# Paired table products, extra dense products and a new order in a gated mix of attention and a state-space convolution

## The chip, the cores and the metric

One Trainium2 chip, one of its cores. The metric is the device time of one execution in microseconds, the median of several runs. The core has five engines that run their own instruction streams and wait for each other by semaphores: TensorE (PE; its weight loads are shown apart as PEld), VectorE (DVE), ScalarE (ACT), GpSimd (POOL) and SyncE (SP). In this kernel POOL and SP do little but issue DMAs.

## What is computed

Two branches over the same input x (2048 x 512) are mixed by a gate per token. Cut to what matters here:

```python
# branch A: 32 heads of 16, 4 segments of 512 tokens
for s in range(4):
    logits = einsum('bhqd,bhkd->bhqk', q[s], k[s]) * scale + mask   # causal
    a_dot = softmax(logits) @ v[s]
    a_mem = (phi(q[s]) @ M) / (phi(q[s]) @ z + 1e-6)
    o[s] = g * a_mem + (1 - g) * a_dot
    M = M + phi(k[s]).T @ v[s];  z = z + phi(k[s]).sum()
a = o @ wo
# branch B: per channel d of 512, a kernel of 2048 taps from 128 complex modes, then a long convolution
l = arange(2048).astype(bfloat16)          # many l fall together
K = einsum('dn,dnl,dn->dl', C, exp(dt * A * l), dt * B).real
y = irfft(rfft(x, 4096) * rfft(K, 4096))[:2048] + x * Dskip
out = sigmoid(x @ gate_w) * a + (1 - sigmoid(x @ gate_w)) * y
```

## The kernel before

**A planner writes the order.** The kernel is built as a list of operations, each with an engine, an estimated cost, tiles that it reads and writes and a key. A list scheduler (`schedule`) takes on each engine, among the operations that can start within 0.12 us, the one with the lowest key; `ORDER` holds for each tag a number that is added to the key, and a second that is added only where DVE competes for an eviction. An eviction (`evac`, lines 324, 325, 327, 328) may go to ACT or DVE. All instructions are then written out engine by engine, with no loops. Every product goes through one helper, line 820.

**Attention.** 4 segments, 4 head groups of 8 heads each, and two halves of a head group: 32 calls of `group`, each with 5 score steps, 160 in all. A score step writes 1024 columns in two PSUM banks (0 and 1, or 2 and 3); ACT takes the exponential of all of it (line 1169). The causal mask of the diagonal blocks is set in one of two ways, a bit in `MASKS` for each step: by two more products, one per bank, that add `negm` through the identity, or by a DVE product with `mask01` after the exponential (line 1178). A step has 2 or 4 diagonal blocks of 128.

**Tables.** The taps of the state-space kernel are made from powers: 20 powers `F` and 32 powers `G` per mode and channel, so that each of 640 exponents is one of F plus one of G. `tables(c)` handles 128 channels, four times over. DVE makes F and G by complex multiplication (lines 1328, 1330, 1333). Then, per channel, PE multiplies G's 32 columns (stationary) with F's 20 columns (moving), summed over the modes, the real and the imaginary part in turn. Four channels stand side by side in the array's columns, so each product is 32 x 20. Results gather in one PSUM bank for each half of the channels, are evicted into `kex`, and four DMAs per table carry `kex` into `KTT`, which has exponents in its partitions.

**Convolution.** A transform of 4096 points in two levels. The first level of x (`x_level1`) is a product with `W1T` and goes through DRAM (`scr_Z`). In `tail`, 16 steps `K0` to `K15` each take the transform of the taps (a product of a matrix from DRAM with `KTT`, so all four tables must be there), that of x, multiply them on DVE (lines 1425, 1427, 1430) and transform back into `V2`. When all of `V2` is there, the last stage `fin` multiplies it with `G2T`, adds branch A, scales and writes out (line 327).

**Memory.** PSUM banks 4 to 7 serve one bank at a time for everything but the scores. `kex` shares its place with `pb2`, a parameter that the preparation reads last in `cbB` (line 936).

Of the kernel before, what the change touches and what calls it, by code (L numbers as in the profile page):

```python
# [16 lines left out]
    'c_ident': (-302.654696, 118.5323), 'c_mk': (25.0776717, 31.1201), 'c_negm': (117.240337, 15.88946),  # L17
    'c_mask': (82.9696732, 148.73681), 'c_ones': (219.06097, 69.01982), 'c_W1': (101.972009, -1.91191),
    'c_G2': (152.510402, 64.12832), 'ld0': (-159.6066, -3.90904), 'ld1': (-178.483329, -24.17737),
    'ld2': (-92.104013, -32.87557), 'ld3': (-67.6677276, 9.94046), 'ld4': (-16.8975543, -9.33976),  # L20
    'ld5': (-4.87843354, -20.81767), 'ldt': (-255.221528, 18.97994), 'ldw0.3': (-120.015437, 20.25449),
    'ldw0.4': (-107.069287, 54.02795), 'ldw0.5': (-74.7706898, 55.68128), 'ldw50': (143.580885, 71.64248),
    'ldbd': (146.873282, -3.63178), 'ldc': (75.9548493, -139.44835), 'prep': (241.088944, 76.53782),
    'xT0': (-135.794939, 94.16918), 'powA0': (-118.34783, 47.94242), 'powA1': (293.056234, 56.59733),
    'powA2': (35.605867, 26.1545), 'powA3': (85.9672701, 3.55388), 'powA4': (-134.9878, 64.48103),
    'powA5': (-26.1625064, 59.29796), 'powA6': (-133.006553, -36.0664), 'powA7': (-142.410857, 92.25773),
    'powA8': (-143.096642, 54.65219), 'powA9': (-10.832777, 2.7911), 'cbA': (-135.566534, 76.23563),
    'powB0': (-38.6484402, 86.47076), 'powB1': (5.73197339, 19.09463), 'powB2': (-13.5842481, 50.52935),
    'powB3': (-134.626625, -55.3453), 'powB4': (-158.321758, -62.26012), 'powB5': (-189.375726, 81.95324),
    'powB6': (-80.3854645, -2.33938), 'powB7': (-23.5296877, 39.40937), 'powB8': (-69.1011372, 80.90111),  # L30
    'powB9': (-110.631611, 11.18354), 'cbB': (-43.7416241, -8.34436), 'gate0': (-83.6885532, -16.32166),
    'gate': (1.11235274, 54.68591), 'proj0.0': (-19.4170356, -12.54463), 'tok0': (-79.3938344, 28.87985),
    'state0': (2.03704365, 1.9988), 'grp0.0.0': (-9.77190791, 56.39033), 'grp0.0.1': (-15.5684214, 42.32006),
    'oph0.0': (16.6476846, 20.40017), 'proj0.1': (-31.4882721, 74.16452), 'grp0.1.0': (-22.0475879, 127.40729),
    'grp0.1.1': (-23.8762151, 61.87469), 'oph0.1': (-9.68776635, -98.76067), 'proj0.2': (13.8209713, 33.73148),
    'grp0.2.0': (-3.0729207, -42.9295), 'grp0.2.1': (-4.41502647, 85.93088), 'oph0.2': (-0.110628858, -73.44253),
    'proj0.3': (-3.65051527, 62.72309), 'grp0.3.0': (-157.898249, 69.86549), 'grp0.3.1': (15.8097506, 82.05476),
    'oph0.3': (1.58288994, 45.63335), 'oproj0': (-119.328043, -32.2024), 'xT1': (152.351944, 17.87594),
    'proj1.0': (9.25225381, 119.56925), 'tok1': (-10.2534902, 33.782), 'state1': (2.65910208, -104.20105),
    'grp1.0.0': (-90.77533, -81.81367), 'grp1.0.1': (2.11773201, -114.61486), 'oph1.0': (-2.73170943, -41.40325),  # L40
    'proj1.1': (1.88542876, 58.71674), 'grp1.1.0': (-50.654272, 32.17712), 'grp1.1.1': (2.9233842, 75.51506),
    'oph1.1': (-10.8350984, -95.48593), 'proj1.2': (1.82372045, 0.09674), 'grp1.2.0': (-40.190034, 101.48513),
    'grp1.2.1': (6.26606409, 118.92692), 'oph1.2': (-0.686318884, -116.61307), 'proj1.3': (0.240651948, 30.33776),
    'grp1.3.0': (-46.8631087, 31.58558), 'grp1.3.1': (4.26113506, 92.65595), 'oph1.3': (16.5142754, -29.00959),
    'oproj1': (-191.3713, -3.8356), 'xT2': (96.7803542, 126.17717), 'proj2.0': (2.03309827, 56.77169),
    'tok2': (4.1651971, -119.61949), 'state2': (5.77674239, -0.78865), 'grp2.0.0': (-34.2653109, -9.07765),
    'grp2.0.1': (-5.67836684, 97.22657), 'oph2.0': (-250.752907, -56.23876), 'proj2.1': (6.5976729, 122.63846),
    'grp2.1.0': (-4.50294478, 30.38303), 'grp2.1.1': (4.81855669, 106.57043), 'oph2.1': (15.6722872, -167.79793),
    'proj2.2': (-0.107249989, 90.02738), 'grp2.2.0': (-195.487509, 48.11696), 'grp2.2.1': (-5.26881311, 86.02262),
    'oph2.2': (10.7493513, -113.28868), 'proj2.3': (-7.49951321, 95.76044), 'grp2.3.0': (5.83724795, 81.21215),  # L50
    'grp2.3.1': (-32.6003357, 74.62712), 'oph2.3': (-34.0930078, -105.98926), 'oproj2': (-42.4160159, -7.99807),
    'xT3': (290.268696, 20.01374), 'proj3.0': (0.804501688, 7.58942), 'tok3': (5.05705523, 9.43832),
    'grp3.0.0': (-16.6209468, 115.71971), 'grp3.0.1': (-94.3400298, 75.95984), 'oph3.0': (34.3743725, -53.14357),
    'proj3.1': (-5.34871522, 74.39357), 'grp3.1.0': (31.8837621, -11.25205), 'grp3.1.1': (-311.171354, -14.40604),
    'oph3.1': (-107.203104, -69.86356), 'proj3.2': (72.9991952, 27.09956), 'grp3.2.0': (20.1657102, -6.85936),
    'grp3.2.1': (-59.0699755, -14.4919), 'oph3.2': (88.4879918, -147.86965), 'proj3.3': (79.119397, 97.40507),
    'grp3.3.0': (5.32990942, 126.86441), 'grp3.3.1': (61.7741135, -22.60438), 'oph3.3': (-130.287319, -60.50239),
    'oproj3': (-33.6345043, -45.3022), 'tab0': (-0.0762501383, 297.60803), 'tab1': (-3.85305439, 267.74954),
    'tab2': (-0.288638216, 266.94455), 'tab3': (9.72332812, 324.53498), 'xl1': (-134.058337, -22.9888),
    'tailload': (-94.6594205, 59.19368), 'K0': (-16.3376241, 5.32994), 'K1': (44.0845545, -26.15755),  # L60
    'K2': (9.34286849, 3.42233), 'K3': (45.356053, 32.70617), 'K4': (39.7158986, -80.36254),
    'K5': (59.226848, -13.36243), 'K6': (-175.798043, 23.12264), 'K7': (-52.4250027, -83.01271),
    'K8': (-81.0202091, -26.97997), 'K9': (70.2758069, 29.6753), 'K10': (11.2349379, 25.06385),
    'K11': (-5.3357892, -30.98575), 'K12': (-72.5533468, 4.35854), 'K13': (83.6417633, 0.11429),
    'K14': (94.4918388, -109.55134), 'K15': (132.562985, 53.83523), 'fin': (-85.9153477, -15.31372),
    'pre0': (169.976104, -25.42423), 'fin0': (91.9347751, 60.72191), 'pre1': (-73.3504102, -61.54381),
    'fin1': (115.799027, 117.99035), 'fin2': (125.104546, 66.48059), 'fin3': (213.962257, 170.74892),
}
MASKS = [2, 0, 0, 0, 0, 0, 0, 0, 0, 28, 0, 0, 0, 1, 0, 0, 16, 16, 14, 4, 0, 28, 0, 1, 3, 15, 31, 31, 15, 13, 26, 20]
# [566 lines left out]
def dft_const():  # L636
    lq = (np_bf16_bits(np.arange(2048, dtype=np.float32)).astype(np.uint32) << 16).view(np.float32).astype(np.int64)
    where = {}
    for f, fe in enumerate(F_EXP):
        for g, ge in enumerate(G_EXP):  # L640
            assert fe + ge not in where
            where[fe + ge] = (f % 5, 4 * g + f // 5)
    assert set(lq[1:].tolist()) == set(where)
    D = np.zeros((128, 16, 5, 2, 128))
    t = np.arange(16)[:, None, None]
    pi = np.arange(2)[None, :, None]
    q = np.arange(64)[None, None, :]
    f = (2 * t + pi + 64 * q).reshape(16, 128)
    for l in range(1, 2048):
        kt, r = where[int(lq[l])]  # L650
        ph = 2 * np.pi * (((2 * f + 1) * l) % 8192) / 8192
        D[r, :, kt, 0, :] += np.cos(ph)
        D[r, :, kt, 1, :] -= np.sin(ph)
    return D


def build_kernel(nc, A_x, A_wq, A_wk, A_wv, A_wo, A_beta, B_A_re, B_A_im, B_B_re, B_B_im,
                 B_C_re, B_C_im, B_log_dt, B_Dskip, gate_w, out):
    with contextlib.ExitStack() as es:
# [102 lines left out]
        kexP = mkpool("kex", 1280, 2)  # L762
# [3 lines left out]
        assert a <= 207 * 1024, a  # L766

        pbP = mkpool("pb", 1024, 2)
# [9 lines left out]
        pb2P = mkpool("pb2", 1024, 1, 0)  # L778
        a = GP.addr
# [182 lines left out]
        def x_level1(xjP, zsP):  # L962
            S.tag = "xl1"
            for qd in range(4):
# [3 lines left out]
                for bl in range(4):  # L968
# [3 lines left out]
                    def f(e, P=P, xj=xj, bl=bl):  # L972
                        for hf in range(2):
                            i = mm(e, ap(P, hf * 512, n=512), ap(W1T, hf * 128, n=128), ap(xj, bl * 512, n=512), True, True)
# [159 lines left out]
        def group(s, hg, gi):  # L1134
# [12 lines left out]
            for si, ent in enumerate(slots):  # L1147
# [3 lines left out]
                def f(e, P=P, ent=ent, md=md):  # L1151
                    dg = {0: [], 1: []}
                    for (hh, J, bk, off) in ent:
# [13 lines left out]
                o_ = op("PE", (0.28 if len(ent) == 2 else 0.36) if md else (0.38 if len(ent) == 2 else 0.63), f, r=[qT, kT, ko, ident, negm], w=[P], acq=[pT], act=0.08 + (0 if md else 0.0533 * len(ent)))  # L1167
# [131 lines left out]
        def tables(c):  # L1299
# [62 lines left out]
            for hf in range(2):  # L1362
# [210 lines left out]
```

## Time and profile before

| | |
|---|---|
| median of 8 runs | 361.13 us |
| lowest, highest | 354.11, 365.34 us |
| the profiled execution | 360.26 us |
| its span, first to last instruction | 358.5 us |
| instructions | 8296 |
| PE busy | 301.8 us, 3409 products |
| weight loads | 126.1 us, 3409 |
| DVE busy | 275.0 us, 667 |
| ACT busy | 286.3 us, 387 |
| mean granted clock of TensorE | 0.931 |

Busy time of PE is from modelled ends, so a busy PE need not be at its peak. The granted clock is the share of full speed that the chip allowed TensorE; it has its own row. In a row of a group, the number after x is the count, then come the busy time in us, the mean of one in ns, the idle time before them, and what ended most of that idle time. "Issue" as a releaser means that nothing in the profile explains the wait. The chain of waits is followed back from the last instruction to what released each step. Most of it is attention and tables up to about 240 us, then attention of the last segment mixed with the 16 steps of the tail up to 338 us, then the last stage.

### The profile page before, as it was taken

The page shows a single profiled execution, that of the slowest core. Times are in us where ns is not written, and L with a number is a line of the kernel's source. Part 1 is how long each engine was busy: PE and PEld are TensorE (multiplying, and loading weights), DVE is VectorE, ACT ScalarE, POOL GpSimd, SP SyncE. Part 2 cuts the span into 40 slices and gives each one's busy share as a digit, 9 for nine tenths or more (in the row PEclk, how much of TensorE's full clock was granted, in tenths as well). Part 3 has the DMA queues.
Part 4 walks back from the last instruction along what each step waited for, and adds up shares of the span by engine and source line. Part 5 has one row for each costly group of instructions (what it writes and reads, how often), then busy time and mean ns, then how long its engine had stood idle before and what let it go on. Part 6 is the DMA issues. An engine that isn't in the chain of part 4 may idle for free.

```text
span 358.5 us, 8296 instructions
## 1 busy us (share of the span) xinstructions
PE 301.8 (84%) x3409; PEld 126.1 (35%) x3409; DVE 275.0 (77%) x667; ACT 286.3 (80%) x387; POOL 17.2 (5%) x39
## 2 busy tenths in 40 slices
PE   0569887788849989989798999969999999999581
PEld 0223332233424433534335433443343333344240
DVE  2689999999848997399996999913686787986320
ACT  2688999999928998989998898926899768665472
POOL 2000000000100000000020000000001121100000
PEclk9996998599988996999999999995899999999997
DMA  7968021023692555410024210251126657443342
GB/s 145 195 147 121 1 90 29 3 58 120 192 123 90 152 143 188 140 35 15 2 87 125 64 44 16 46 165 35 37 49 229 216 152 237 140 121 89 106 155 92
DMA packets 43118, 37.56 MB, mean 105 GB/s; under 512 B 30569, under 2 KB 35945, under 8 KB 42217
## 3 DMA queue, kind: packets, MB, share of 16 engines
q1 hardware_dynamic: 39016, 22.18, 24.6%
q0 software_dynamic: 2720, 13.63, 12.4%
q10 hardware_dynamic: 1344, 1.21, 1.7%
q8 instruction: 27, 0.44, 0.5%
q14 instruction: 11, 0.08, 0.1%
HBM read 17.74 MB, written 9.44 MB: 76 GB/s over the span
## 4 chain that ended last, share of the span: by engine, by line
PE 35%; DVE 31%; ACT 23%; DMA 4%; issue 4%; SPq 0%
PE psum L820 35%; ACT sb L1169 12%; ACT sb L324 6%; DVE sb L325 4%; DVE sb L1333 4%; DVE sb L1330 4%; DVE sb L1328 4%; DMA sb<-in_B_A_im_dram 2%; ACT sb L327 2%; DVE sb L1232 1%; DVE sb L1430 1%; DVE sb L1252 1%; DVE sb L1425 1%; DMA sb<-scr_obuf 1%; DMA sb<-sb 1%
## 5 line engine op out<-in xcount | busy, mean ns | idle before, releaser
L820 PE MATMUL psum<-sb 128*32 128x20 bf16 (+13 forms) x3233 | 290.8, 278 | 48.3 <-DMA sb<-in_A_x_dram 12.6
L820 PEld LDWEIGHTS psum<-sb 128*128 128x128 bf16 (+4 forms) x3233 | 115.7, 97 | 219.1 <-issue 91.1
L1169 ACT ACTIVATE sb<-psum 128x1024 bf16<-128x1024 f32 x160 | 157.7, 1037 | 9.8 <-PE psum L820 9.3
L324 ACT ACTIVATE sb<-psum 128x512 bf16<-128x512 f32 (+2 forms) x134 | 97.8, 754 | 38.7 <-PE psum L820 37.9
L325 DVE CAST sb<-psum 128x512 bf16<-128x512 f32 (+2 forms) x39 | 35.0, 897 | 17.2 <-PE psum L820 17.1
L1328 DVE TENSOR_TENSOR sb<-sb 128x512 bf16<-128x512 bf16 (+3 forms) x52 | 34.3, 664 | 0.1
L1333 DVE TENSOR_TENSOR sb<-sb 128x512 bf16<-128x512 bf16 (+3 forms) x52 | 34.0, 664 | 0.1
L1330 DVE TENSOR_TENSOR sb<-sb 128x512 bf16<-128x512 bf16 (+3 forms) x52 | 33.9, 664 | 0.0
L1178 DVE TENSOR_TENSOR sb<-sb 128x512 bf16<-128x512 bf16 (+1 forms) x43 | 15.8, 372 | 5.3 <-ACT sb L1169 5.2
L324 ACT ACTIVATE sb<-sb 128x256 bf16<-128x256 bf16 (+1 forms) x32 | 15.4, 499 | 1.1 <-DVE sb L904 1.0
L1425 DVE TENSOR_TENSOR sb<-sb 128x1024 bf16<-128x1024 bf16 x16 | 10.8, 683 | 6.5 <-ACT sb L324 5.2
L1229 DVE RECIPROCAL sb<-psum 128x32 f32<-128x32 bf16 x16 | 5.7, 355 | 11.6 <-PE psum L1226 11.6
L1430 DVE TENSOR_TENSOR sb<-sb 128x512 bf16<-128x512 bf16 x32 | 13.2, 418 | 0.6
L317 POOL DMA_DIRECT2D sb<-c_D x16 | 8.6, 537 | 95.3 <-PE psum L820 70.4
L327 ACT ACTIVATE sb<-psum,sb 128x512 bf16<-128x512 f32 x13 | 8.6, 687 | 4.8 <-PE psum L820 4.8
L1427 DVE TENSOR_TENSOR sb<-sb 128x1024 bf16<-128x1024 bf16 x16 | 10.9, 684 | 0.2 <-ACT sb L324 0.2
L1232 DVE TENSOR_TENSOR sb<-psum,sb 128x512 bf16<-128x512 bf16 x16 | 10.9, 684 | 0.0
L1226 PE MATMUL psum<-sb 128*128 128x128 bf16 x128 | 10.3, 226 | 0.1
L1252 DVE TENSOR_TENSOR sb<-psum,sb 128x256 bf16<-128x256 f32 x24 | 9.2, 417 | 0.1
L1226 PEld LDWEIGHTS psum<-sb 128*128 128x128 bf16 x128 | 7.8, 100 | 2.9 <-issue 1.1
L325 DVE COPY sb<-sb 128x256 bf16<-128x256 bf16 x17 | 4.0, 250 | 5.9 <-PE psum L820 5.9
L1125 ACT ACTIVATE sb<-sb 128x512 bf16<-128x512 bf16 x12 | 8.0, 662 | 0.1
(71 smaller groups left out, 143.5 us busy)
## 6 DMA issues: line engine op xcount, KB each, us to landing
sb<-c_D POOLq DMA_DIRECT2D x16, 320.0 KB, 4.4
scr_Z<-sb SPq DMA_DIRECT2D x16, 256.0 KB, 2.0
sb<-scr_Z POOLq DMA_DIRECT2D x4, 1024.0 KB, 5.5
sb<-sb SPq DMA_DIRECT2D x15, 256.0 KB
sb<-in_A_x_dram POOLq DMA_DIRECT2D x4, 512.0 KB, 5.1
scr_obuf<-sb SPq DMA_DIRECT2D x12, 128.0 KB, 1.9
scr_abuf<-sb SPq DMA_DIRECT2D x12, 128.0 KB, 1.8
sb<-scr_abuf SPq DMA_DIRECT2D x3, 512.0 KB, 6.0
```

Source lines behind the costliest of these rows:

```text
L324: fa = lambda e: e.activation(dst(), src(), ACT.Copy)
L325: fd = lambda e: e.tensor_copy(dst(), src())
L327: fa = lambda e: e.activation(dst(), src(), ACT.Copy, scale=scale())
L820: mm = lambda e, o_, l, r_, st, sp, **kw: e.matmul(o_, lhsT=l, rhs=r_, start=st, stop=sp, skip_group_check=True, **kw)
L1169: op("ACT", c_act(1024), lambda e, P=P, pT=pT: e.activation(ap(pT, n=1024), ap(P, n=1024), ACT.Exp, scale=0.25), r=[P], w=[pT])
L1178: o_ = op("DVE", c_tt(128 * len(offs)), lambda e, pT=pT, dims=dims: e.tensor_tensor(ap(pT, dims=dims + [[1, 128]]), ap(pT, dims=dims + [[1 ...
L1226: i = e.transpose(ap(P, tb * 256 + gi * 128, n=128), ap(ra[gi], tb * 128, n=128), ap(ident, n=128))
L1232: op("DVE", c_dps(512), lambda e: e.tensor_tensor(ap(o1, dims=[[128, 4], [16, 8], [1, 16]]), ap(P, dims=[[256, 4], [32, 8], [1, 16]]), ap( ...
L1328: op("DVE", ct, lambda e: e.tensor_tensor(run(tile, ne, dst, 1), run(tile, ne, src, sstep), pwv(0), ALU.mult), r=rd + [pw], w=wr + [tile])
L1330: op("DVE", ct, lambda e: e.tensor_tensor(run(t2, n, 0, 1), run(tile, ne, src, sstep), pwv(1), ALU.mult), r=rd + [pw], w=[t2])
L1333: op("DVE", max(c_tt(256 * n), 0.4), lambda e: e.tensor_tensor(D_(), D_(), ap(t2, n * 128, [[-n * 128, 2], [2 * n, 64], [1, 2 * n]]), ALU. ...
L1430: op("DVE", c_tt(512), lambda e, Y=Y, Tt=Tt, c=c, alu=alu: e.tensor_tensor(ap(Y, 512 * c, n=512), ap(Y, 512 * c, n=512), ap(Tt, 512 * c, n ...
```

## The change

Four things are changed.

1. `tables` multiplies two channels at once: 64 columns of G (two channels) with 40 columns of F (the same two channels), two such products side by side in the array. Of each 64 x 40 result only the two blocks of 32 x 20 on its diagonal are used. A table's 32 steps go into three PSUM banks (12, 12 and 8 steps) and not two, each with a tag and key of its own, and groups of four steps have keys 0.6 apart. The eviction takes all 40 columns; the DMA picks the blocks. `kex` is twice as large, and `pb` moves into its place. So that channels lie as the pairs need them, three constants and the moving operands of the products with `W1T` and `G2T` are rearranged.
2. `FILLS`: 44 score steps begin with one more product, 128 rows of `kT` by 512 columns of `qT`, whose result is overwritten by the score products that follow.
3. `MASKS` has other bits: 71 steps are masked on DVE, before 43.
4. Every number in `ORDER` is new.

```diff
 ORDER = {
-    'c_ident': (-302.654696, 118.5323), 'c_mk': (25.0776717, 31.1201), 'c_negm': (117.240337, 15.88946),
...
+    'c_ident': (-730.92885, 77.11646), 'c_mk': (-104.472085, 70.23437), 'c_negm': (83.1023139, 57.29774),
...
+    'oproj3': (-215.379276, -234.39235), 'tab0': (-3.31108379, 556.81397), 'tm0.0': (-175.547175, 364.57757),
...
-MASKS = [2, 0, 0, 0, 0, 0, 0, 0, 0, 28, 0, 0, 0, 1, 0, 0, 16, 16, 14, 4, 0, 28, 0, 1, 3, 15, 31, 31, 15, 13, 26, 20]
+MASKS = [1, 0, 0, 0, 0, 0, 8, 1, 29, 1, 17, 18, 0, 31, 18, 7, 26, 3, 8, 31, 4, 26, 31, 23, 10, 13, 30, 25, 30, 23, 20, 14]
+FILLS = [0, 0, 2, 0, 10, 15, 0, 11, 29, 1, 20, 16, 27, 16, 25, 20, 0, 0, 0, 0, 14, 2, 5, 0, 0, 4, 10, 17, 4, 0, 13, 1]
...
-            where[fe + ge] = (f % 5, 4 * g + f // 5)
+            where[fe + ge] = (f // 4, 4 * g + f % 4)
...
-        kexP = mkpool("kex", 1280, 2)
+        kexP = mkpool("kex", 2560, 2)
...
-        pbP = mkpool("pb", 1024, 2)
...
         pb2P = mkpool("pb2", 1024, 1, 0)
+        pbP = mkpool("pb", 1024, 2, 0)
...
-                            i = mm(e, ap(P, hf * 512, n=512), ap(W1T, hf * 128, n=128), ap(xj, bl * 512, n=512), True, True)
+                            i = mm(e, ap(P, hf * 512, n=512), ap(W1T, hf * 128, n=128), ap(xj, bl * 512, [[2, 2], [4, 128], [1, 2]]), True, True)
...
+                    if FILLS[gidx] >> si & 1:
+                        mm(e, ap(P, n=512), ap(kT, n=128), ap(qT, n=512), True, True)
...
-            for hf in range(2):
+            for pc, (lo_, n_) in enumerate(((0, 12), (12, 12), (24, 8))):
+                S.tag = "tm%d.%d" % (c, pc)
                 P = S.ps()
-                for sl0 in range(0, 16, 4):
-                    def f(e, P=P, hf=hf, sl0=sl0):
-                        for sl in range(sl0, sl0 + 4):
+                for s0 in range(0, n_, 4):
+                    S.key = k0 + KEYS[3] * 0.8 + 8 * pc + 0.6 * s0
+
+                    def f(e, P=P, lo_=lo_, s0=s0):
+                        for sl in range(s0, s0 + 4):
                             for cc in range(2):
-                                for dq in range(4):
-                                    dl = 32 * dq + 16 * hf + sl
-                                    i = mm(e, ap(P, sl * NF, n=NF, p0=32 * dq, np_=32), ap(G, (1 - cc) * GPL + (dl // 2) * 2 * NG + dl % 2, [[2, NG]]),
-                                           ap(F, cc * FPL + (dl // 2) * 2 * NF + dl % 2, [[2, NF]]), cc == 0, cc == 1, tile_position=(0, 32 * dq))
+                                for ct in range(2):
+                                    j, par = 32 * ct + (lo_ + sl) // 2 * 2, sl % 2
+                                    i = mm(e, ap(P, sl * 2 * NF, n=2 * NF, p0=64 * ct, np_=64), ap(G, (1 - cc) * GPL + j * 2 * NG + par, [[2, 2 * NG]]),
+                                           ap(F, cc * FPL + j * 2 * NF + par, [[2, 2 * NF]]), cc == 0, cc == 1, tile_position=(0, 64 * ct))
                         return i
...
-                S.evac(lambda hf=hf: ap(kex, 16 * hf, [[32, NF], [1, 16]]), lambda P=P: ap(P, dims=[[1, NF], [NF, 16]]), 320, r=[P], pw=[kex])
+                S.evac(lambda lo_=lo_, n_=n_: ap(kex, lo_, [[32, 10], [320, 4], [1, n_]]), lambda P=P, n_=n_: ap(P, dims=[[4, 10], [1, 4], [2 * NF, n_]]), 40 * n_, r=[P], pw=[kex])
...
-                      lambda dq=dq: ap(kex, n=640, p0=32 * dq, np_=32), 40960, r=[kex], pw=[KTT], rate=60e3, issue=0.6)
+                      lambda dq=dq: ap(kex, dq % 2 * 160, [[320, 4], [1, 160]], p0=32 * dq, np_=32), 40960, r=[kex], pw=[KTT], rate=60e3, issue=0.6)
...
-                            i = mm(e, ap(P, n=512), ap(G2T, kt * 128, n=128), ap(V2, (b4 * 2 + kt) * 512, n=512), False, kt == 1)
+                            i = mm(e, ap(P, n=512), ap(G2T, kt * 128, n=128), ap(V2, (b4 * 2 + kt) * 512, [[2, 128], [256, 2], [1, 2]]), False, kt == 1)
```

## The prediction

> **What bounds it now.** I read the page first: share by engine, the 40 slices, the chain of waits by line. No single engine is the limit (PE 84%, ACT 80%, DVE 77%), so the question is which stage waits for what. Then the groups by shape on PE, the chain in order of time, and stages cut out by time.
>
> ```profile
> PE   0569887788849989989798999969999999999581
> ...
> DVE  2689999999848997399996999913686787986320
> ACT  2688999999928998989998898926899768665472
> ...
> PEclk9996998599988996999999999995899999999997
> ...
> PE 35%; DVE 31%; ACT 23%; DMA 4%; issue 4%; SPq 0%
> ```
>
> A digit covers 9.0 us. Up to slice 26 (234 us) DVE and ACT are nearly always full. Counted from 0, there are two holes in both: slice 11 (DVE 4, ACT 2 tenths) and slice 26 (1 and 2), each followed by a granted clock under full. The chain names the holes (start, length, what was on it):
>
> ```profile
> 98.65 1.65 PE psum L820 x126
> 100.30 4.82 issue
> 105.12 8.65 PE psum L820 x40
> ...
> 134.45 10.72 PE psum L820 x151
> ...
> 227.39 10.65 PE psum L820 x297
> 238.04 3.48 issue
> 241.52 4.58 PE psum L820 x31
> 246.10 0.97 PE psum L1226 x8
> 247.07 10.01 PE psum L820 x45
> ```
>
> "Issue" is PE waiting for nothing the trace shows, straight after a burst of hundreds of products. Groups by shape say what they are:
>
> ```profile
> L820 PE MATMUL psum<-sb 128*32 128x20 bf16 x1024 | 12.0, 176 | 4.3 <-issue 4.0 <-DVE sb L1333 0.2
> ```
>
> These are the table products. By the records of this line they run in bursts of 32, some 6 to 10 ns apart, 8.4 us in all. So they cost PE little as work, but they are 2048 of its 6818 instructions (one weight load and one product each). The page's q8 row has 27 instruction blocks in 0.44 MB, so 16 KB and about 253 PE instructions each. A burst uses up a block in about 1.2 us. In the packet records the block that ended the first stall moved from 102.75 to 103.71, and PE went on at 105.12; for the second it moved from 239.14 to 240.15, and PE went on at 241.52. I read both stalls as PE out of instructions.
>
> The stages (PE busy, weight loads, DVE, ACT, POOL, granted clock, DMA share, GB/s):
>
> ```profile
> 59.87:70.11 10.24, 7.77 (x50) 2.37 (x50) 10.24 (x25) 10.24 (x17) 0.00 (x0) 0.50 0.07 15
> 97.42:104.25 6.83, 2.23 (x141) 1.42 (x140) 3.37 (x9) 3.55 (x7) 0.53 (x1) 1.00 1.10 140
> 104.25:111.07 6.82, 5.95 (x21) 1.92 (x22) 4.49 (x13) 2.84 (x4) 0.00 (x0) 0.50 0.21 63
> ...
> 134.97:141.80 6.83, 6.83 (x65) 1.98 (x62) 5.46 (x17) 5.12 (x8) 0.53 (x1) 0.50 0.53 162
> ...
> 240.78:254.43 13.65, 12.91 (x84) 4.63 (x85) 4.78 (x15) 8.08 (x10) 0.00 (x0) 0.50 0.09 23
> 342.60:350.80 8.20, 8.20 (x39) 3.50 (x36) 2.25 (x3) 7.46 (x12) 0.00 (x0) 1.00 0.51 190
> ```
>
> The clock is 1.00 or 0.50 and changes in steps of 3.41 us. I weighed each 3.41 us by the array it used (columns streamed times the share of rows and columns, at 0.21 us for a full product of 512, from 39 in 8.20 us above). Each fall to 0.50 between 25 and 255 us came after a step with at most 1.31 us of such dense work (0.38, 1.31, 0.00, 1.05, 0.09); the lowest step that kept the clock had 1.20. Attention before 100 us lives at 1.2 to 1.9, just above.
>
> **The holes, as prices.** A, 238.04 to 254.43: the stall 3.48 plus half of the 12.91 us at half clock, 9.9. B, 100.30 to 111.07: 4.82 plus half of 5.95, 7.8. C, 134.97 to 141.80: half of 6.83, 3.4. D, 59.87 to 70.11: ACT is full there; PE is on the chain only from 67.36, so half of 2.75, 1.4. Sum 22.5.
>
> **Table products in pairs (`tables`).** 1024 products of 32x20 become 512 of 64x40, half of each result unused. At 6 to 10 ns each they cost 3.1 to 5.1 us against 8.4; on the chain stand 1.65 us and some 3.5 us of the 10.65, so about 2.5 us go. PE's instructions fall by 1024, and the eight emitted groups of a table hold 32 instructions, not 64, with keys 0.6 apart per four products. Masks and fills included, PE has 6818 - 1024 + 88 - 112 = 5770. Two of four tables (142 to 151 us, 188 to 196 us) already ran without a stall at twice the density, so I take both stalls as gone, and with them the empty steps that cost the clock: A and B in full, 17.7. If PE were not short of instructions, only the halved bursts would remain.
>
> The Trainium skill speaks against this: "Runtime: NRT & Kernel Launch", section "Instruction fetch mechanics", says that streaming in 16 KiB blocks is mostly hidden behind issue. The trace shows two stalls, 8.3 us, so I follow the trace; by the page the forecast would be 8.3 higher.
>
> **Evictions of the tables.** Two of 320 elements become 480, 480, 320. Rows: 320 takes 439 ns on ACT, 512 takes 618; 480 lies at 588 in between. A table goes from 0.88 to 1.62 us, four of them +2.9 us. The strip of 320 bytes that each DMA to `KTT` now reads changes neither count nor size (16, 40 KB, 2.2 us to landing); three of four tables land long before use, so nothing. `pb` under `kex` adds a wait on `cbB`, ended by 76.5 us (last L936), before the first product at 92: nothing; `pb2` already made it.
>
> **Masks.** 43 steps masked on DVE become 71: 13 more with two blocks (285 ns, L1178 128x256) and 15 with four (424 ns): 3.7 + 6.4 = 10.1 us more DVE. PE loses 56 products and 13 x 0.107 + 15 x 0.213 = 4.6 us of dense work. By segment +2, +15, +14, -3.
>
> **Fills.** 44 more 128x512 products, 10, 18, 6, 10 by segment, 0.21 us each at full clock: 9.4 us. In segments 0 to 2 the score step waits for ACT's Exp (1037 ns each, 158 us in all) and the fill lies under it: nothing; it delays the score products behind it by 0.21 us, up to 7.3 us for the 34 if that cover were gone. In segment 3 PE is the bound (9.0 of 9.0 us in most slices): 10 x 0.21 = 2.1, and three masks back on PE, 0.5. What they buy: D and C are falls without a stall. Segments 0 and 1 gain dense work net, segment 2 loses some 1.0 us. I take half of C and D, 2.4.
>
> "TensorE: Matmul & The Clock Gate", Part 1, lets the clock fall after an idle window of 3.4 us. Before 59.87 PE was busy 2.69 of 3.41 us and fell all the same, so the trace goes by dense work; by the page fills buy nothing, 2.4 less gain.
>
> **Where the added work lands.** In 36 to 99, 117 to 135 and 153 to 234 us DVE is 97% and ACT 95% busy. 13.0 us more, shared by choosing the engine of the evictions, is 6.5; all on DVE alone 13; in the holes, nothing. I take 6.5: it is nearest to those rows. Cap: in 99 to 117 and 135 to 153 the two engines idle 23.9 us together, so B and C can give back at most 12.
>
> **Rearranged columns.** The products with `W1T` and `G2T` now read pairs of elements 8 or 512 bytes apart. No row has that. The table products read single elements at 4 byte steps, 32 of them (four abreast) in 0.2 us, so 20 columns in at most 25 ns: at worst a third of full rate, 0.43 us more per 512. The 32 with `G2T` lie on the last 9 us: 0 to 13.6 us. Below zero is excluded, since the same columns stream. I take 0: `KTT` is read in pieces too and PE's pace there is normal.
>
> **New order.** All keys change; no row prices that. It moves DMAs on SP and POOL as well, and it may open new steps under 1.3. I take one more fall of D's kind, 1.4; bounds are none and C's 3.4 twice.
>
> **Sum.** On the profiled 360.26 us (span 358.5): -17.7 - 2.4 - 2.5 + 6.5 + 2.6 + 1.4 = -12.1, so 348.2. The median shown, 361.13, is 0.9 higher: 349.
>
> **Rivals.**
> 1. No change: the gaps close, but DVE takes all 13.0 us, and C and D stay with two falls of C's kind instead of one of D's: -17.7 - 2.5 + 13.0 + 2.6 + 6.8 = +2.2, about 361 to 363; with half of that, 357 and up. For it: DVE is on 31% of the chain, with runs of 20 us and more. Against: the evictions can move, and 39 on DVE (35.0 us) is more than enough to move.
> 2. Slower: a spread group keeps its PSUM bank, one of the four (4 to 7) for everything but the scores, from its first product to its eviction. 12 such holds; PE's waits for evictions on these banks (L324, L325, L1232, L1252) are 22 us between 36 and 241. If one missing bank doubles them while it is held for T, the price is 22 x 12T/205 = 1.3T. From T = 12 us it eats the forecast and more; at 14 us, 18 more, 367. For it: banks are waited for. Against: keys inside a group differ by 2.4 at most, where a whole attention group has 11.
> 3. Slower: rearranged reads at their bound, 349 + 13.6 = 363, and with the fills uncovered 370.
> 4. The change doesn't do what it says: the stalls come from busy DMA queues (share 1.10 in 97 to 104 us), not density; A and B keep their 8.3: 357.
>
> **Chances.** Forecast, with rival 4 mostly below the bound, 0.72; rival 1, 0.12; rival 2, 0.10; rival 3, 0.06. A measurement tells about 1% (3.6 us) from no change. Faster 0.72, same 0.12, slower 0.16. Range: everything recovered and all additions hidden is 361.1 - 22.5 = 338.6; the upper end takes in rivals 4 and 1 and the bound of the reads, 364. The forecast's own cases lie at 338 to 357.
>
> **What would show it.** Right: no "issue" piece over 1 us on the chain, slices like 11 and 26 gone from DVE and ACT, clock 1.00 after the table products; table products x512; ACT and DVE together near 574 us. Wrong: stalls elsewhere with the clock full; half clock in segment 2, where fills are few; waits of PE for L324 and L325 clearly over 22 us; the last products with `G2T` more than 0.21 us apart.

## The result and the profile after

The changed kernel takes 360.37 us (median of 11 runs, 358.46 to 365.34), the kernel before 358.15 us (median of 32). The ratio is 1.0108, 95% interval 1.0066 to 1.0151: slower by about 1%, where 349 us and faster had been forecast. A second set of runs gave 1.0101 (1.0027 to 1.0174). The ratios, here and below, set a kernel's fast runs (within 1.5% of its fastest) against fast runs of the kernel before, so they can differ from the quotient of the two medians, which is 1.006 here. The profiled execution took 361.58 us.

The page after, first the span, then rows of the 40 slices, then the chain by engine:

```profile
span 359.7 us, 7273 instructions
...
DVE  2689999889989999889985999697599878896020
ACT  2688999889898998689977988589776488555362
...
PEclk9996998589999999589965999599999999999798
...
DVE 41%; PE 40%; ACT 11%; DMA 4%; issue 2%; SPq 0%; ACTq 0%
```

The holes of before are gone: slice 11 has 8 tenths on DVE and 9 on ACT, slice 26 has 9 and 7. But the clock has new falls, at slices 16, 20 to 21 and 25. On the chain DVE has gone from 31% to 41%. Cut out by time, with the columns of the tables of stages above (busy time by engine, granted clock, DMA):

```profile
60.10:73.80 13.70, 12.19 (x69) 3.58 (x67) 12.65 (x31) 11.60 (x20) 0.00 (x0) 0.50 0.05 11
145.40:155.70 10.30, 10.30 (x70) 3.56 (x70) 8.14 (x20) 5.79 (x7) 0.00 (x0) 0.50 0.28 26
183.00:196.60 13.60, 13.60 (x145) 6.37 (x143) 7.69 (x23) 9.34 (x12) 0.00 (x0) 0.50 0.29 79
223.90:234.20 10.30, 10.01 (x36) 2.69 (x34) 6.97 (x24) 6.53 (x10) 0.00 (x0) 0.50 0.12 26
336.60:343.40 6.80, 4.88 (x13) 1.42 (x11) 0.75 (x1) 1.37 (x2) 0.00 (x0) 0.50 0.17 62
```

With the first fall (26.0 to 32.8) that is 61 us at half clock, against 44 in the profile of before, and in three of these rows PE is busy without a break while DVE and ACT are not. On the chain they are long pieces of PE (start, length):

```profile
145.32 3.92 PE psum L823 x37
149.24 0.54 PE psum L1075 x4
149.78 8.05 PE psum L823 x46
...
184.04 11.61 PE psum L823 x99
...
224.47 11.80 PE psum L823 x45
...
339.79 12.29 PE psum L823 x42
```

The ends of equal work in the two traces show the lead won and lost. Of the 160 exponentials the 48th ends 6.6 us later than before and the 56th 2.4 us earlier (the first stall); the 80th is 5.4 late, the 128th 6.2 late, the 136th 6.4 early (the second stall). After that attention and tail are mixed differently in the two kernels: the products of `K3` to `K8` lead by 11 to 14 us, that of `K15` by 2.7, and the last stage, its first part at half clock, loses those.

The pieces of "issue" on the chain are small now, and the table products take hardly less of PE. First the largest of such pieces, then the group by shape:

```profile
312.57 1.11 issue
```

```profile
L823 PE MATMUL psum<-sb 128*64 128x40 bf16 x512 | 11.1, 191 | 0.2 <-DVE sb L1340 0.2
```

By the records of the group the 512 products run some 16.3 ns apart at full clock, 8.6 us in all (start to start, gaps under 0.1 us); the 1024 of before take 7.6 counted so, and 8.4 by the prediction's count.

### The profile page after: what moved, and what is told of

Read it like the earlier page. It is cut to its first block, busy times and chain, and to the rows that moved or that the text cites. A ratio compares the mean times of both kernels' runs of the same rounds, so it can differ in the third digit from the quotient of the medians.

```text
span 359.7 us, 7273 instructions
## 1 busy us (share of the span) xinstructions
PE 313.0 (87%) x2885; PEld 128.2 (36%) x2885; DVE 291.4 (81%) x708; ACT 281.1 (78%) x378; POOL 17.3 (5%) x39
## 4 chain that ended last, share of the span: by engine, by line
DVE 41%; PE 40%; ACT 11%; DMA 4%; issue 2%; SPq 0%; ACTq 0%
PE psum L823 39%; ACT sb L1176 6%; DVE sb L1340 6%; DVE sb L1335 5%; DVE sb L1337 5%; DVE sb L330 5%; ACT sb L329 4%; DVE sb L1185 3%; DMA sb<-in_B_A_im_dram 2%; DVE sb L1239 2%; DVE sb L1259 1%; DMA sb<-sb 1%; DVE sb L1236 1%; DVE sb L916 1%; DVE sb L1079 1%
## 5 line engine op out<-in xcount | busy, mean ns | idle before, releaser
L823 PE MATMUL psum<-sb 128*128 128x512 bf16 (+15 forms) x2709 | 301.9, 308 | 37.1 <-DMA sb<-in_A_x_dram 12.5
L823 PEld LDWEIGHTS psum<-sb 128*128 128x128 bf16 (+4 forms) x2709 | 117.2, 102 | 217.0 <-issue 97.7
L329 ACT ACTIVATE sb<-psum 128x512 bf16<-128x512 f32 (+2 forms) x123 | 89.5, 749 | 33.8 <-PE psum L823 32.8
L330 DVE CAST sb<-psum 128x512 bf16<-128x512 f32 (+3 forms) x54 | 47.4, 882 | 17.3 <-PE psum L823 17.3
L1185 DVE TENSOR_TENSOR sb<-sb 128x512 bf16<-128x512 bf16 (+1 forms) x71 | 25.7, 366 | 7.1 <-ACT sb L1176 7.0
L329 ACT ACTIVATE sb<-sb 128x256 bf16<-128x256 bf16 (+1 forms) x31 | 15.1, 501 | 1.1 <-DVE sb L330 0.9
L333 DVE TENSOR_SCALAR sb<-psum,sb 128x512 bf16<-128x512 f32 x3 | 2.3, 751 | 12.5 <-PE psum L823 12.5
L1239 DVE TENSOR_TENSOR sb<-psum,sb 128x512 bf16<-128x512 bf16 x16 | 11.0, 687 | 0.2
L1259 DVE TENSOR_TENSOR sb<-psum,sb 128x256 bf16<-128x256 f32 x24 | 9.2, 411 | 0.0
L916 DVE TENSOR_TENSOR sb<-sb 128x256 f32<-128x256 f32 x18 | 7.6, 422 | 0.6 <-ACT sb L914 0.6
```

The costliest lines, as they stand in the source:

```text
L329: fa = lambda e: e.activation(dst(), src(), ACT.Copy)
L330: fd = lambda e: e.tensor_copy(dst(), src())
L823: mm = lambda e, o_, l, r_, st, sp, **kw: e.matmul(o_, lhsT=l, rhs=r_, start=st, stop=sp, skip_group_check=True, **kw)
L1185: o_ = op("DVE", c_tt(128 * len(offs)), lambda e, pT=pT, dims=dims: e.tensor_tensor(ap(pT, dims=dims + [[1, 128]]), ap(pT, dims=dims + [[1 ...
L1239: op("DVE", c_dps(512), lambda e: e.tensor_tensor(ap(o1, dims=[[128, 4], [16, 8], [1, 16]]), ap(P, dims=[[256, 4], [32, 8], [1, 16]]), ap( ...
L1259: op("DVE", c_dps(256), lambda e, hb=hb: e.tensor_tensor(ap(o2, hb * 256, [[128, 2], [16, 8], [1, 16]]), ap(P2, hb * 512, [[136, 2], [17, ...
```

## The experiments

"Same order" means that every engine's instructions stand as in the kernel named, and only the part shown differs. Otherwise the planner lays the work anew from the keys. The table gives medians over all runs, 4 to 11 of each, with the median granted clock; the ratio is to the kernel before, run on the same chip.

| kernel | us | clock | ratio (95%) |
|---|---|---|---|
| changed | 360.4 | 0.913 | 1.011 (1.007 to 1.015) |
| pair_only | 354.9 | 0.936 | 0.992 (0.985 to 1.000) |
| pair_order | 366.6 | 0.894 | 1.011 (1.001 to 1.021) |
| after_nofill | 363.0 | 0.876 | 1.018 (1.010 to 1.026) |
| after_wide | 355.2 | 0.948 | 0.997 (0.993 to 1.002) |
| before_wide | 363.5 | 0.956 | 1.021 (1.016 to 1.027) |
| masks_back | 356.9 | 0.949 | 0.996 (0.992 to 1.000) |
| dve_light | 350.7 | 0.942 | 0.975 (0.966 to 0.984) |
| after_plainv2 | 359.4 | 0.912 | 1.010 (1.004 to 1.016) |
| before_dvelight | 356.9 | 0.938 | 1.002 (0.996 to 1.008) |
| before_masks | 381.1 | 0.882 | 1.062 (1.047 to 1.077) |
| before_masks_back | 374.2 | 0.922 | 1.036 (1.025 to 1.046) |
| pair_fix | 353.0 | 0.944 | 0.982 (0.975 to 0.989) |
| wide_fix | 354.2 | 0.946 | 0.995 (0.988 to 1.001) |
| pair_fill0 | 354.0 | 0.951 | 0.983 (0.973 to 0.993) |
| dve28 and dve28_b, 10 runs | 356.4 | 0.918 | none given |
| after_again | 361.5 | 0.913 | 1.010 (1.003 to 1.017) |
| wide_dve28 | 353.5 | 0.944 | 0.990 (0.983 to 0.997) |

The kernel before ran at a median clock of 0.93 to 0.95. Within a kernel the time goes with the clock of the run: over 19 runs of before on each of three chips, 2.5 to 2.9 us more for each 0.01 less, and over 20 of the changed kernel 2.1 us. At equal clock the changed kernel is the faster one: on the chip where both ran again, before took 358.9 and 361.4 us at 0.927 and 0.928, the changed kernel 357.2 at 0.924.

**The parts alone.** `pair_only` takes the changed kernel with the old order numbers, the old masks and no fills.

```diff
-S.tag = "tm%d.%d" % (c, pc)
+S.tag = "tab%d" % c        # and ORDER, MASKS of before, FILLS all 0
```

> The kernel before with the paired table products alone (old order numbers, old masks, no fills; each of the new table tags takes the old number of its table). Theory 1, clock: pairing takes the two 'issue' stalls (8.3 us) and the empty steps behind them away, and what the whole change lost again comes from masks and order; so this is faster than before by 5 to 12 us, with no 'issue' piece over 1 us. Theory 2, pairing itself is the loss (round time of the array, evictions, rearranged reads): within 2 us of before or slower. Theory 3, order: neither, because new costs make the planner lay the work anew; then the sign is open and the half-clock time differs by more than 10 us from before's 44.

It gained 2.8 us (0.8%), less than the 5 to 12 of theory 1; the interval, nothing to 5.4 us, doesn't tell it from theory 2's 2 us. The two stalls are gone, as theory 1 said (the longest "issue" piece left is 1.10 us, elsewhere): the stages that held them run at full clock.

```profile
58.80:75.90 17.10, 14.74 (x76) 4.45 (x74) 17.10 (x43) 14.47 (x24) 0.00 (x0) 0.50 0.04 9
97.00:117.00 20.00, 18.74 (x228) 8.98 (x228) 12.65 (x33) 17.72 (x26) 0.53 (x1) 1.00 0.41 116
234.00:254.00 20.00, 19.48 (x285) 9.85 (x285) 15.17 (x45) 18.18 (x26) 1.07 (x2) 1.00 0.49 153
```

The fall near 60 us has grown from 10.2 to 17.1 us instead, and four of 3.4 us have come, so half-clock time is 38 us against 44. VectorE is on 36% of the chain, before on 31%, and busy for 281.1 us against 275.0.

`pair_order` keeps pairing and old masks and takes the new order numbers.

```diff
-MASKS = [1, 0, 0, 0, 0, 0, 8, 1, 29, ...]; FILLS = [0, 0, 2, 0, 10, ...]
+MASKS = [2, 0, 0, 0, 0, 0, 0, 0, 0, 28, ...]; FILLS = [0] * 32
```

> Paired tables and the new order numbers, with the old masks and no fills. Against pair_only (0.992 of before) it is the order alone. Theory 3, the order is the loss: 1.01 of before or more, granted clock 0.92 or less. Theory 1, masks took the dense work: within 0.5% of pair_only and granted clock 0.93 or more.

1.011 against 0.992: theory 3, the order is the loss, and the clock goes with it. The four runs took 361.6, 363.5, 369.7 and 369.9 us at clocks of 0.911, 0.902, 0.881 and 0.886; pair_only's five fastest have a median clock of 0.942. So the two shorter runs are some 0.035 lower, and by pair_only's own runs (2.0 us for each 0.01) that is 7 us: an estimate, but as much as the ratios differ by. The profile is of the 369.7 us run and so shows the loss at its largest: 82 us at half clock by the clock's records, where the two shorter runs' clocks would make it some 60. Its stages:

```profile
50.00:80.00 30.00, 25.87 (x168) 7.99 (x167) 29.27 (x76) 26.91 (x41) 0.53 (x1) 0.72 0.15 46
100.00:160.00 60.00, 56.34 (x639) 25.93 (x638) 50.08 (x120) 48.81 (x67) 1.58 (x3) 0.81 0.46 134
160.00:200.00 40.00, 38.82 (x413) 15.55 (x412) 30.50 (x63) 34.36 (x43) 2.79 (x6) 0.86 0.13 41
```

From 100 to 200 us PE is the fullest engine of the three, and in this run it has 0.81 and 0.86 of its clock.

**Fills, in the changed kernel's order.** `after_nofill` leaves the 44 extra products out; `after_wide` puts 72 elsewhere; `before_wide` puts the same 72 into the kernel before.

```diff
-if FILLS[gidx] >> si & 1:
+if False:                            # after_nofill
+if s < 3 and si in (0, 2, 4):        # after_wide, before_wide
```

> The changed kernel with its 44 extra dense products left out, all instructions else in the same order. Theory 1, clock: more steps of 3.41 us fall under 1.3 us of dense work, half-clock time up from 61 us, time the same or up by as much as 5 us. Rival, the fills only load PE: 44 x 0.21 = 9.4 us less on PE, time down by 2 to 9 us.

> The changed kernel with the extra dense product in the first, third and fifth score step of every group of segments 0 to 2 (72 in place of 44, none in segment 3), same order. Theory 1, clock: granted clock 0.95 or more, four of the falls between 60 and 235 us gone or shorter, time down by 5 to 12 us. Rival, VectorE is the bound: time within 2 us, whatever the clock does.

> The kernel before with the same 72 extra dense products, same order. Theory 1, clock: the falls at 60 and 135 us go, those behind the two stalls (104 and 241 us) stay because PE has nothing to run there; 2 to 5 us faster. Rival, fills only load PE: 72 x 0.21 = 15.3 us more PE, 3 to 10 us slower.

Between `after_nofill`, the changed kernel and `after_wide` nothing differs but dense products, and the clock goes 0.876, 0.913, 0.948, the time 363.0, 360.4, 355.2. More work on PE makes the kernel faster. The 44 products are worth about 2.6 us (the two intervals overlap), 72 in other places another 5 (they don't). Of the stretches shown above after_wide has these left:

```profile
58.90:72.50 13.60, 12.27 (x70) 3.63 (x69) 12.53 (x31) 12.30 (x21) 0.00 (x0) 0.50 0.06 13
147.60:154.50 6.90, 6.85 (x38) 2.13 (x40) 5.19 (x11) 4.48 (x7) 0.00 (x0) 0.51 0.01 3
```

The falls at 183 and 224 us are gone, where PE had been the only full engine. That is theory 1 at the low end of its range. In the kernel before the rival won: clock up by 0.01, and 2% slower. Half-clock time did shrink there: the falls at 104 and 135 us went and that behind the second stall shrank from 13.7 to 6.8 us. But PE's waits for instructions stay, as "issue" pieces of 1.33, 1.72, 1.28 and 3.43 us on the chain, and 15 us of products must be paid.

**Masks and VectorE.** `masks_back` lets PE mask again in the steps that had moved to VectorE (46; 18 others moved to PE, so 28 net, which is what the expectations count; PE then masks 135 steps, before 117), with VectorE's product cut to one element; `dve28` only cuts it in those 46 steps (`dve28_b` is the same kernel again, `after_again` the changed kernel beside it); `dve_light` cuts all 71, `before_dvelight` the 43 of before.

```diff
-def f(e, P=P, ent=ent, md=md, si=si):
+def f(e, P=P, ent=ent, md=bool(md and MASKS0[gidx] >> si & 1), si=si):  # masks_back
...
-e.tensor_tensor(ap(pT, dims=dims + [[1, 128]]), ..., ap(mask01, ...), ALU.mult)
+e.tensor_tensor(ap(pT, offs[0] + 127, n=1), ap(pT, offs[0] + 127, n=1), ap(mask01, 127, n=1), ALU.mult)
```

> The changed kernel, same order, but in the score steps that the change took from PE's masking to VectorE's, PE adds the mask again by its two products, and VectorE's product stays as one of a single element (so its place in the order is kept). Theory 1, clock: PE's dense work is back, granted clock up from 0.913 to 0.93 or more, 3 to 6 us faster than the changed kernel. Theory 2, VectorE is the bound: some 7 us less on VectorE, faster too, but at the same clock. Rival, neither: within 1.5 us.

> The changed kernel, same order, with every one of VectorE's 71 mask products cut to one element; it leaves out that part of the causal mask. VectorE loses 71 x 0.2 = 14 us, PE nothing, so the dense work is as it was. Theory 2, VectorE is the bound: 6 us faster or more. Theory 1, clock: a gain of under 4 us, clock within 0.01 of the changed kernel's 0.913.

> Control for dve_light: the kernel before, same order, with VectorE's 43 mask products cut to one element; it leaves out that part of the causal mask. 43 x 0.2 = 8.6 us less on VectorE. If VectorE is a bound of the stage in both kernels, 4 to 8 us faster (dve_light gave 12.8 for 14 us). If it is only the change that made VectorE the bound, under 2 us.

> The changed kernel, same order, with VectorE's mask product cut to one element in only those score steps that the change moved to it; it leaves out that part of the causal mask, and PE adds nothing. Against masks_back (0.996 of before, changed kernel 1.011) this lacks PE's mask products alone. If the gain of masks_back was VectorE's 7 us, the time is that of masks_back or less (PE has 4.6 us less): 0.985 to 0.996. If it was PE's dense work and the clock: 1.005 or more, granted clock near 0.915.

> dve28 once more (its four runs lay between 346 and 363 us), beside the changed kernel on one chip; it leaves out VectorE's part of the mask in the 28 moved steps. VectorE's 7 us as the cause: 4 us or more faster than the changed kernel, as masks_back was (5.3). PE's missing dense products as the cause: within 2 us of it and a granted clock within 0.01 of its.

> The changed kernel as it is, on the same chip: 1.011 of before, granted clock 0.913.

dve_light went from 1.011 to 0.975. The group of mask products in the changed kernel, and in dve_light:

```profile
L1185 DVE TENSOR_TENSOR sb<-sb 128x512 bf16<-128x512 bf16 (+1 forms) x71 | 25.7, 366 | 7.1 <-ACT sb L1176 7.0
```

```profile
L1186 DVE TENSOR_TENSOR sb<-sb 128x1 bf16<-128x1 bf16 x71 | 10.8, 155 | 8.1 <-ACT sb L1176 7.4
```

14.9 us less in this group (VectorE's busy time is 12.0 us less) gave 10 us by the medians and 13 by the ratios, and the clock rose by 0.03 though PE's instructions are the same. The expectation that the clock would stay fell: what VectorE holds back also empties PE's steps. One case in the changed kernel's waits, from 139 to 147 us, just ahead of the fall at 145.4:

```profile
PE psum L823 <- DVE sb L1081: 2.6, 1, 2.6
```

The same cut in the kernel before gave nothing (1.002). So it is the change that made VectorE's mask products count. dve28's first four runs lay from 346 to 363 us; with six more its median is 356.4 at clock 0.918, against 361.5 (20 runs, with after_again) at 0.913 for the changed kernel. These runs scatter too widely for a ratio, but they follow the clock closely, so equal clocks can be compared: at 0.910 and 0.911 dve28 took 357.7 to 359.5 us, the changed kernel at 0.911 361.6 to 362.1. That is 3 to 4 us at equal clock, 5 by the medians, for the 7.0 us of VectorE's time (284.4 against 291.4) in the moved steps alone. masks_back has much the same time (356.9, on another chip) at clock 0.949, with PE's products to pay. So the moved masks act through VectorE's time; PE's missing dense products seem to cost clock, and giving them back to cost PE as much.

> dve28 with the 72 fills of after_wide (same order; the same part of the mask left out). If fills and VectorE's time act through the same thing, the clock, the second adds little: within 2 us of the better of the two, granted clock 0.95 to 0.97. If they act apart, the gains add: 5 us by the fills, 4 to 5 by VectorE, 0.985 of before or less.

On the chip where the changed kernel took 361.5 us and dve28_b 356.4, this took 353.5: 8.0 us less, where dve28_b gave 5.1 and after_wide, on another chip, 5.2. That is between the two expectations: the causes overlap in part. That both fill PE's empty steps is the likely reason; it wasn't tried by itself.

**Masks in the old order.**

```diff
-MASKS = [2, 0, 0, 0, 0, 0, 0, 0, 0, 28, ...]     # open order: the planner lays anew
+MASKS = [1, 0, 0, 0, 0, 0, 8, 1, 29, ...]        # before_masks
```

> The kernel before (tables not paired, old order numbers, no fills) with the new masks alone: VectorE +10 us, PE's dense work -4.6 us; the planner lays the work anew. If masks lower the clock and load VectorE: granted clock under 0.93 and 3 to 8 us slower. If the order numbers alone are to blame: within 2 us of before.

> before_masks (1.061 of before) with PE masking again where the new masks had taken it away and VectorE's product there cut to one element, so the work is nearly that of before and the order that of before_masks. If the masks themselves cost the 6%: 1.00 to 1.02. If it is the order that the planner makes of old numbers and new costs: 1.045 or more.

6% slower, far beyond either expectation. With the masks given back in that same order it is 3.6%, again between the two expectations: by the two ratios more than half of the loss is the order that the planner makes of old numbers and new costs, the rest the masks. (The work isn't quite that of before: PE masks 135 steps, and VectorE keeps 46 products of one element, 0.16 us each.) A few changed costs are enough to move this kernel by more than the change itself.

**The last stage.** `after_plainv2` reads `V2` straight, so the output's columns lie in another order. `pair_fix` and `wide_fix` do it with the columns put right by the eviction, in pair_only and in after_wide.

```diff
-ap(G2T, kt * 128, n=128), ap(V2, (b4 * 2 + kt) * 512, [[2, 128], [256, 2], [1, 2]])
+ap(G2T, kt * 128, n=128), ap(V2, (b4 * 2 + kt) * 512, n=512)
-ap(ident, n=128), ap(aj, b4 * 512, n=512)
+ap(ident, n=128), ap(aj, b4 * 512, [[2, 2], [4, 128], [1, 2]])               # *_fix
-S.evac(..., lambda P=P: ap(P, n=512), 512, ...)
+S.evac(..., lambda P=P: ap(P, dims=[[2, 128], [256, 2], [1, 2]]), 512, ...)   # *_fix
```

> The changed kernel with the last stage reading V2 straight, so that the output's columns lie in another order. Its 32 products go from 270 to 216 ns: 32 x 0.054 = 1.7 us faster than the changed kernel by any theory; if within 0.5 us, the evictions set the end and the reading is hidden.

> pair_only with the last stage mended: V2 is read straight and the evictions from PSUM put the columns in their places instead. Same order. Reading at 216 in place of 270 ns would give 1.7 us if the evictions keep their 0.69 us; if the strided reading of PSUM costs them 0.1 us or more each, nothing or a loss. After_plainv2 gave 0.4 us by the medians and 2 at equal clock.

> after_wide (72 fills, changed kernel's order, 0.997 of before) with the same mend of the last stage: 0.990 to 0.995 of before if the reading is worth 1 to 2 us; 0.997 or more if it isn't.

The timeline of PE's last products, the changed kernel's and then after_plainv2's (start, length):

```profile
339.79 12.28 PE L823 MATMUL psum<-sb 128*128 128x512 bf16 x42 [1.92 <-DMA sb<-sb]
```

```profile
336.67 10.91 PE L823 MATMUL psum<-sb 128*128 128x512 bf16 x42 [1.88 <-DMA sb<-sb]
```

By the records the `G2T` products stand 270 ns apart at full clock with the rearranged reading, 216 straight: 32 x 0.054 = 1.7 us. At half clock both stand some 430 ns apart, and in the changed kernel's profile nine of the 32 ran so, which leaves 1.2 us. after_plainv2's medians show 0.9 us, its ratio 0.4, unclear by its interval. pair_fix shows 1.0% against pair_only, on another chip and with overlapping intervals, wide_fix nothing that its interval can tell. ACT's evictions read PSUM in pairs at no price (687 ns in both). pair_fix has the lowest ratio of the kernels that compute it all: 0.982 of before.

> pair_fix (0.982 of before) with the extra dense product in the first, third and fifth score step of segment 0 (24 in all), same order. Its profile falls to half clock for 17 us from 58.8. If the fall goes: granted clock 0.96 or more and 2 to 4 us faster, 0.971 to 0.976. If ACT sets that stage anyway: within 1 us, as the fills of before_wide cost more than they gave.

The clock is 0.951 with the fills, against 0.944, and the time stays (0.983). The intervals are 1% wide, but it fits the expectation's second case: in the row of that stage above, from 58.8 to 75.9 us, VectorE is busy without a break and ACT for 14.5 of 17.1 us, so a higher clock would buy little there.

## Why the prediction was wrong

The ladder of the parts, each step with its ratio to before: pairing 0.992, with the new order 1.011, with the new masks 1.018, with the fills 1.011. In microseconds of 358: -2.8, +6.7, +2.5, -2.6. The steps come from different chips, and in the first three the planner lays the work anew. By the intervals each is uncertain by 2.6 to 4.6 us, so the first two are clear, if barely, and the last two are not by the ladder alone. The forecast had some -18.7 for the pairing (17.7 and 2.5 gained, half of the 2.9 us of evictions lost) and +1.4 for the order.

- **Holes A and B in full, 17.7, and 2.5 of bursts: the step that failed.** The mechanism was right; neither stall is left. But pairing alone brought 2.8 us. A hole was priced at its whole length, as if nothing else would then set the pace; in pair_only VectorE took a larger part of the chain (36%, before 31%), PE's waits for evictions that rival 2 counts rose from 23 to 31 us, and half-clock time went to other places (38 us, before 44). A further part was eaten by the last stage: with it mended the pairing is worth 1.8%, 6.4 us. The table products take PE 8.6 us, not 3.1 to 5.1. The prediction took the price of a product to stay as it was, but what costs is a round of products side by side, and there are 256 rounds before (1024 by four) and after (512 by two). No run pairs the products in the order of before, so how much of the missing 16 us is the planner's new layout stays open.
- **New order: the second step that failed.** It was priced at one fall of 1.4 us, at most two of C's kind, 6.8. It costs 6.7, with some 4 us of doubt, and the clock goes with it: 0.942 in pair_only's fastest runs, 0.911 and 0.902 in pair_order's two shorter ones. "No row prices that" was true, and the likeliest value should then not have stood at the cheap end.
- **Where the added work lands: about right.** Masks were to add 10.1 us to VectorE; the group went from 15.8 to 25.7. Half of the added time was counted; dve28 gave back 3 to 5 us for 7.0 us of VectorE, so 0.5 to 0.7 of it. ACT and DVE together are 572.5 us (574 forecast), an eviction of 480 is 589 ns (588).
- **Fills: right in sign, too small.** 2.4 us were counted as their gain and 2.1 as their price, 0.3 net; leaving them out costs 2.6 net, with some 3 us of doubt, and other places bring another 5. That fills in segment 0 lie under ACT and VectorE fits pair_fill0, which gains nothing by them and loses nothing.
- **Rearranged reads: taken as nothing, up to 1.7 us.** The bounds held (0 to 13.6), the value did not; the pieces of `KTT` that were the reason are 64 bytes long, not 4.
- **The weighing by dense work** had one reading wrong: the lowest step that kept the clock was not at 1.20 but at 0.71 us, from 97.4 to 100.8 us, by the starts of its products. It is the step with 126 table products in 1.65 us on the chain, so the weight of such small products is in doubt; all other steps there that kept the clock had 1.18 or more, and the falls came after 1.29 or less.
- **The signs.** Signs of being right came: slices 11 and 26 are filled, ACT and DVE are as forecast, and the longest "issue" piece, 1.11 us, is hardly over the 1 us named. But two of being wrong came too: half clock in segment 2 (183 to 197 us) and `G2T` products 0.27 us apart.
- **Rival 1** named the right engine, but its place was not the evictions; that its 361 to 363 us are near the measured 360.4 is in part luck, for it counted the holes at 17.7 too. **Rival 2**, the PSUM banks: PE's waits for L330, L329, L1239 and L1259 between 36 and 241 us are 18 us in the changed kernel, before 23 with the smallest rows counted in, so its sign didn't come. **Rival 4**, busy DMA queues and not density: in pair_only the queues were busy from 97 to 104 us too (share 0.75), without a stall. In before_wide four "issue" pieces over 1 us ended 1.3 to 1.5 us after the packet of an instruction block had landed, as both stalls of before did (1.4), so PE was short of instructions.
- **Two pages of the Trainium skill.** "Runtime: NRT & Kernel Launch", section "Instruction fetch mechanics", holds fetching hidden: with half the instructions it is (1.11 us at most), at two instructions in 6 to 10 ns it was not (4.82). "TensorE: Matmul & The Clock Gate", Part 1, speaks of idle windows. The falls after the change follow steps of 0.22 to 1.30 us of dense work, and in three of the six PE was busy for 2.6 to 3.1 of the 3.41 us; and the row of three kernels in one order, 0.876, 0.913, 0.948, differs in dense products alone.

What stays open, beside the layout of pair_only: why the new order has more steps of low dense work; the experiments show that its clock is lower, not which of its keys make it so.

## What to carry to other kernels

A hole in the profile is worth what its removal leaves as the next limit, and a clock that depends on the work moves the holes: price a fall where the stage around it is bound by that engine; in before_wide and pair_fill0 a higher clock elsewhere bought nothing. Where every place in the order changes, no part's saving can be taken in full; an estimate made of parts should carry the order as its widest term. A part that looks free (a rearranged operand) is checked where it stands alone on the path, which here was the last stage.

## What the runs showed of the hardware

- One kernel's runs differ by up to 18 us (before, 352.3 to 370.7 us on one chip), and the granted clock goes with nearly all of it: correlation -0.97 over 19 runs of before, -0.94 over 12 of the changed kernel.
- Table products with 32 columns of weights and 20 moving ran four in 26 to 33 ns at full clock and 28 in a burst at half clock; with 64 and 40, two in some 33 ns, and 53 at half clock. At 0.21 us for 512 columns the streaming alone would be 8 and 16 ns. So a round has a floor, and half the products in as many rounds took as long.
- PE stood for 1.3 to 4.8 us after bursts of table products (two instructions each in 6 to 10 ns) until a 16 KB block of instructions had landed, six times in before and before_wide; with half as many instructions it didn't.
- A moving operand in pairs of elements costs: 216 ns straight, 237 with pairs 8 bytes apart (`W1T`), 270 with 512 (`G2T`), medians at full clock; at half clock straight and `G2T` reads both took some 430.
